# Summing 512 columns of A's part of the last row tile ahead of B's row tiles, and holding the sum in PSUM

## The chip, the cores and the metric

One core of a Trainium2 chip. The metric is the device time of one execution in microseconds; "span" is the same execution as the trace sees it, about 1.5 us shorter. TensorE does the matrix products and adds them up in PSUM, a memory of eight banks; ScalarE and VectorE read finished sums out of it (an "eviction") into SBUF, the working memory; the SyncE and ScalarE queues issue transfers (DMA).

## The reference, cut to what matters

```python
g = sigmoid((x * gate_w).sum(-1, keepdims=True))
a = linear_attention(x, A_wqkv, A_wo)      # 2048 x 640, 32 heads of 20
b = linear_attention(x, B_wqkv, B_wo)
return g * a + (1 - g) * b
```

Each attention block ends in a product with an output weight. The kernel folds each block's key-value sums into that weight (WPA, WPB, 640 x 640), so that its last stage is, for each of 16 row tiles of 128 rows, a product of scaled queries with WPA plus one with WPB.

## The kernel before

The output stage. `o_mm` adds one block's part of one row tile to PSUM: five contraction steps, each a 128x512 matmul and, for the full width of 640, a 128x128 one.

```python
def o_mm(X, t, ps, lo, hi, first="A", last="B"):
    ...
            for g in range(NC):                        # NC = 5
                for l0 in range(lo, hi, 512):
                    r = e.matmul(a[:, l0-lo : h0-lo], PQ[X, b][:, g, ...], WP[X][:, g, l0:h0],
                                 start=(X == first and g == 0), stop=(X == last and g == NC - 1))
    op("PE", fn, ..., ins=[bfx[X, b, t % 4 // 2]] + bwpm[X], outs=[ps], ...)   # waits for WP[X]

def o_part(t):      # A's part of a row tile, then ScalarE copies it to SBUF (OA)
    ps, b = Buf("oa", "ps", 2), Buf("oas")             # two PSUM banks
    o_mm("A", t, ps, 0, D, last="A")
    op("ACT", lambda e: e.activation(OA[t], psw(ps, D), ACT.Copy), ..., name="oac")

def o_rest(t):      # B's part, then VectorE adds OA and the row tile is stored
    ps = Buf("o", "ps", 2)
    o_mm("B", t, ps, 0, D, first="B")
    o_post(t, ps, 0, D, "ADD")
```

Row tiles 0 to 14 are done in these two passes, because WPB comes late: it is computed, stored to DRAM and loaded back in another layout. Row tile 15 is done in one go at the end, A and B into one sum:

```python
def out_last(t):
    for lo, hi, eng in ((0, 512, "ACT"), (512, D, "DVE")):
        ps = Buf("o", "ps")                            # one PSUM bank
        for X in XS:                                   # A, then B
            o_mm(X, t, ps, lo, hi)
        o_post(t, ps, lo, hi, eng, ...)

...
wp_burst("B", 0)
o_part(5)
o_part(6)
wp_burst("B", 1)      # second half of WPB; its store and the load follow
o_part(7)
for t in range(8, NOA):    # NOA = 15
    o_part(t)
...
for t in range(NOA):
    o_rest(t)
...
out_last(NT - 1)
```

A small scheduler inside the kernel orders the other engines' work and deals out the eight PSUM banks; TensorE's order is the program's.

## Time and profile before

| | us |
|---|---|
| time, median of the first three runs | 188.17 (188.03 to 188.83) |
| span of the profiled execution | 186.8 |
| TensorE busy | 184.0 (98%) |
| WPB: load issued, landed | 156.62, 161.35 |
| TensorE's first matmul of B | 161.49 |

The lines stand in the prediction below. Read them so: in a kernel whose TensorE is busy nearly all the time, look for the places where it stands still. Once it does so in the output stage, between A's last matmul and B's first, until WPB lands.

### The profile page before, as it was taken

Reading aid. Unit: us, or ns where it says so; the run is one execution under the profiler, and the core shown is the slowest. Engines: PE = TensorE matmul, PEld = TensorE weight load, DVE = VectorE, ACT = ScalarE, POOL = GpSimd, SP = SyncE. Lnnn points to the kernel's source line nnn. Section 1 sums busy time; section 2 is a strip of 40 time slices with the busy share of each in tenths; the row PEclk is TensorE's granted clock in tenths of the full one; section 3 lists DMA queues with packets and bytes.
Section 4 is the critical chain, followed back from the end, with each engine's and each line's share of the span. In section 5 each row is a group of like instructions: output and inputs, shape, how many; then the busy total and the mean of one; then the engine's idle time right before and its main releaser. Section 6 shows DMA issues by size and latency. Waiting matters only on the chain.

```text
span 186.8 us, 3273 instructions
## 1 busy us (share of the span) xinstructions
PE 184.0 (98%) x1297; PEld 106.6 (57%) x1297; DVE 137.4 (74%) x264; ACT 95.2 (51%) x167; POOL 0.8 (0%) x10
## 2 busy tenths in 40 slices
PE   9999999999999999999999999999999999999995
PEld 4555555555555556555557555555566555555552
DVE  2388888888833555487799999998899996368652
ACT  5455655556554546544675666887633775300001
POOL 1000000000000000000000000000000000000000
DMA  6999999994001011010701412025426256523433
GB/s 190 291 163 163 266 394 362 338 200 114 4 0 35 0 39 35 0 35 20 100 2 35 84 33 50 14 62 154 175 41 115 58 131 164 143 105 107 142 107 105
DMA packets 36501, 21.38 MB, mean 114 GB/s; under 512 B 25694, under 2 KB 36230, under 8 KB 36486
## 3 DMA queue, kind: packets, MB, share of 16 engines
q1 hardware_dynamic: 36044, 20.96, 44.4%
q8 instruction: 10, 0.16, 0.4%
q10 hardware_dynamic: 442, 0.21, 0.4%
q14 instruction: 5, 0.04, 0.1%
HBM read 10.87 MB, written 4.26 MB: 81 GB/s over the span
## 4 chain that ended last, share of the span: by engine, by line
PE 92%; DMA 4%; ACT 2%; issue 0%; DVE 0%; SPq 0%; DVEq 0%
PE ps L795 23%; PE ps L536 19%; PE ps L641 18%; PE ps L955 18%; PE ps L642 5%; PE ps L537 5%; DMA WPB<-wpsB 3%; DMA wpsB<-WKW 2%; PE ps L703 2%; PE ps L467 1%; ACT WKW L753 1%; PE ps L738 1%; ACT PKB L979 1%; PE ps L480 1%; DVE TSB L999 0%
## 5 line engine op out<-in xcount | busy, mean ns | idle before, releaser
L536 PE MATMUL ps<-WKW,XT 128*128 128x512 bf16 x160 | 44.6, 382 | 0.0
L812 ACT ACTIVATE EK<-ps 128x512 bf16<-128x512 f32 x40 | 23.9, 598 | 30.1 <-PE ps L795 29.9
L537 PE MATMUL ps<-WKW,XT 128*128 128x128 bf16 (+1 forms) x160 | 35.3, 220 | 0.0
L569 ACT ACTIVATE EK<-ps 128x640 bf16<-128x640 f32 x32 | 22.4, 704 | 10.3 <-DVE EK L572 5.4
L536 PEld LDWEIGHTS ps<-WKW,XT 128*128 128x128 bf16 x160 | 15.7, 98 | 19.6 <-DMA WKW<-in_B_wqkv_dram 0.7
L795 PE MATMUL ps<-XT,WQA 128*128 128x512 bf16 x100 | 24.5, 379 | 0.0
L795 PE MATMUL ps<-XT,WQB 128*128 128x512 bf16 x100 | 23.8, 380 | 0.0
L641 PE MATMUL ps<-XN,PKA 128*128 128x512 bf16 x80 | 23.5, 379 | 0.0
L641 PE MATMUL ps<-XN,PKB 128*128 128x512 bf16 x80 | 23.5, 379 | 0.0
L822 DVE TENSOR_SCALAR EK<-EK 128x512 bf16<-128x512 bf16 x40 | 11.6, 289 | 13.5 <-ACT EK L812 13.3
L642 PE MATMUL ps<-XN,PKA 128*128 128x129 bf16 x80 | 17.6, 220 | 0.0
L642 PE MATMUL ps<-XN,PKB 128*128 128x129 bf16 x80 | 17.6, 220 | 0.0
L955 PE MATMUL ps<-WPA,EX 128*128 128x512 bf16 x120 | 17.0, 299 | 0.0
L955 PE MATMUL ps<-WPB,PKA 128*128 128x512 bf16 x120 | 16.5, 299 | 0.3 <-DMA WPB<-wpsB 0.3
L795 PEld LDWEIGHTS ps<-XT,WQB 128*128 128x128 bf16 x100 | 10.9, 118 | 8.6 <-issue 0.4
L537 PEld LDWEIGHTS ps<-WKW,XT 128*128 128x128 bf16 x160 | 15.8, 98 | 0.0
L572 DVE TENSOR_SCALAR EK<-EK 128x640 bf16<-128x640 bf16 x32 | 10.4, 326 | 7.2 <-ACT EK L569 7.1
L795 PEld LDWEIGHTS ps<-XT,WQA 128*128 128x128 bf16 x100 | 10.6, 117 | 8.1
L641 PEld LDWEIGHTS ps<-XN,PKA 128*128 128x128 bf16 x80 | 9.4, 117 | 7.9
L641 PEld LDWEIGHTS ps<-XN,PKB 128*128 128x128 bf16 x80 | 9.4, 117 | 7.9
L580 DVE SCALAR_TENSOR_TENSOR PKA<-ps,EK 128x640 bf16<-128x640 f32 x16 | 13.2, 825 | 0.5
L580 DVE SCALAR_TENSOR_TENSOR PKB<-ps,EK 128x640 bf16<-128x640 f32 x16 | 13.2, 825 | 0.6
(77 smaller groups left out, 222.8 us busy)
## 6 DMA issues: line engine op xcount, KB each, us to landing
out_dram<-TSB SPq DMA_DIRECT2D x15, 160.0 KB, 1.8
XN<-in_A_x_dram SPq DMA_DIRECT2D x1, 2240.0 KB, 8.9
WKW<-in_A_wqkv_dram SPq DMA_DIRECT2D x5, 160.0 KB, 3.9
WKW<-in_B_wqkv_dram SPq DMA_DIRECT2D x5, 160.0 KB, 3.6
WQA<-in_A_wqkv_dram SPq DMA_DIRECT2D x1, 800.0 KB, 10.6
WQB<-in_B_wqkv_dram SPq DMA_DIRECT2D x1, 800.0 KB, 11.7
WVA<-in_A_wqkv_dram SPq DMA_DIRECT2D x1, 800.0 KB, 12.7
WVB<-in_B_wqkv_dram SPq DMA_DIRECT2D x1, 800.0 KB, 14.5
```

Source lines behind the costliest of these rows:

```text
L536: e.matmul(a[:, 0:512], l, WK[X][:, c, 0:512], start=(c == 0), stop=(c == NC - 1))
L537: return e.matmul(a[:, 512:w], l, WK[X][:, c, 512:w], start=(c == 0), stop=(c == NC - 1))
L569: op("ACT", lambda e: e.activation(EK[:, ek.slot, :], psw(ps, D), ACT.Exp), act_cost(D), ins=[ps] + first, outs=[ek], name="ke")
L572: lambda e: e.tensor_scalar(EK[:, ek.slot, :], EK[:, ek.slot, :], 1.0, EPS, op0=ALU.min, op1=ALU.add),
L580: lambda e: e.scalar_tensor_tensor(PKt[X][:, t, :], psw(ps, D), 0.0, EK[:, ek.slot, :], op0=ALU.max, op1=ALU.add),
L641: e.matmul(a[:, 0:512], l, XN[:, t, 0:512], start=(t == 0), stop=(t == NT - 1))
L642: return e.matmul(a[:, 512 : D + 1], l, XN[:, t, 512 : D + 1], start=(t == 0), stop=(t == NT - 1))
L703: r = e.matmul(PS[0:n, ps.slot, GR * i : GR * i + NC * w], WV[X][:, c, lo : lo + n], gv[:, c, :, 24 * u : 24 * u + w], start=(c == 0), sto ...
L795: r = e.matmul(PS[:, ps.slot, :], WQ[X][:, c, g::5], XT[:, c, 512 * b : 512 * b + 512], start=(c == 0), stop=(c == NC - 1),)
L812: lambda e: e.activation(EQ[:, eq.slot, :], PS[:, ps.slot, :], ACT.Exp),
L822: lambda e: e.tensor_scalar(EQ[:, eq.slot, :], EQ[:, eq.slot, :], 1.0, EPS, op0=ALU.min, op1=ALU.add),
L955: r = e.matmul(a[:, l0 - lo : h0 - lo], PQ[X, b][:, g, 128 * (t % 4) : 128 * (t % 4) + 128], WP[X][:, g, l0:h0], start=(X == first and g = ...
```

## The change

Its intent is to give TensorE something to do in that gap. A's part of row tile 15 needs no WPB; its 512-column piece is summed ahead of B's first row tile, and the sum stays in its bank until B's part is added.

```diff
-    def out_last(t):
-        for lo, hi, eng in ((0, 512, "ACT"), (512, D, "DVE")):
-            ps = Buf("o", "ps")
-            for X in XS:
-                o_mm(X, t, ps, lo, hi)
+    LAST = ((0, 512, "ACT"), (512, D, "DVE"))
+    blast = [Buf("o", "ps") for _ in LAST]
+
+    def last_a(t):
+        o_mm("A", t, blast[0], 0, 512)
+
+    def last_b(t):
+        for (lo, hi, eng), ps in zip(LAST, blast):
+            if hi == D:
+                o_mm("A", t, ps, lo, hi)
+            o_mm("B", t, ps, lo, hi)
             o_post(t, ps, lo, hi, eng, "ACT" if hi == D else "SP")
 ...
     for t in range(8, NOA):
         o_part(t)
+    last_a(NT - 1)
 ...
-    out_last(NT - 1)
+    last_b(NT - 1)
```

## The prediction

> **What bounds the kernel now.** I read the page's engine shares first, then the chain that ended last, then the waits in the last 30 us, and then the timeline around the two places that the diff touches. The page says that TensorE is nearly never free, and where the output matmuls (line 955) stand:
>
> ```profile
> PE 184.0 (98%) x1297; PEld 106.6 (57%) x1297; DVE 137.4 (74%) x264; ACT 95.2 (51%) x167; POOL 0.8 (0%) x10
> ...
> L955 PE MATMUL ps<-WPA,EX 128*128 128x512 bf16 x120 | 17.0, 299 | 0.0
> L955 PE MATMUL ps<-WPB,PKA 128*128 128x512 bf16 x120 | 16.5, 299 | 0.3 <-DMA WPB<-wpsB 0.3
> ```
>
> The last number of each row is idle time just before the group. A's output matmuls never wait. B's wait once, for the transfer that loads WPB, B's folded output weights. The chain that ended last, in order of time (start, us, what), passes through exactly that transfer:
>
> ```profile
> 152.88 3.61 DMA wpsB<-WKW
> ...
> 156.62 4.73 DMA WPB<-wpsB
> 161.35 0.14 issue
> 161.49 23.27 PE ps L955 x170
> ...
> 184.84 0.29 DVE TSB L999
> ```
>
> So the end is set by: WPB stored to DRAM and loaded back, landing at 161.35; 0.14 us until TensorE's first B matmul at 161.49; then TensorE without a pause to the last matmul; then an eviction and the last output transfer. Work that does not need WPB and can run before 161.49 is worth at most the hole that TensorE has there. How big is the hole? The views say 0.28, but that counts from a matmul's end. I take starts instead, from narrow cuts of the timeline (start, us, engine, line, operation, count):
>
> ```profile
> 160.99 0.22 PE L955 MATMUL ps<-WPA,PKA 128*128 128x128 bf16 x1
> ...
> 161.49 0.38 PE L955 MATMUL ps<-WPB,PKA 128*128 128x512 bf16 x1 [0.28 <-DMA WPB<-wpsB]
> ...
> 181.86 0.38 PE L955 MATMUL ps<-WPA,PKA 128*128 128x512 bf16 x1
> ```
>
> The first is the last matmul of A's row tile 14, the second the first of B's row tile 0, the third the first of the last row tile. Fifteen row tiles of five (512 + 128) pairs lie between the second and the third: 20.37 us, 1.358 a tile, 0.272 a pair.
>
> The end of the kernel in the timeline:
>
> ```profile
> 181.86 1.24 PE L955 MATMUL ps<-WPA,PKA 128*128 128x512 bf16 x5
> ...
> 182.94 1.24 PE L955 MATMUL ps<-WPB,GSA 128*128 128x512 bf16 x5
> 182.98 2.25 SPq L354 DMA_DIRECT2D out_dram<-TSB  x2
> ...
> 184.02 0.44 PE L955 MATMUL ps<-WPA,PKA 128*128 128x128 bf16 x5
> ...
> 184.28 0.60 ACT L1001 ACTIVATE TSB<-ps 128x512 bf16<-128x512 f32 x1 [22.32 <-PE ps L955]
> 184.30 0.44 PE L955 MATMUL ps<-WPB,GSA 128*128 128x128 bf16 x5
> 184.84 0.29 DVE L999 CAST TSB<-ps 128x128 bf16<-128x128 f32 x1 [1.89 <-PE ps L955]
> 185.17 0.35 ACTq L354 DMA_DIRECT2D out_dram<-TSB  x1
> ```
>
> From the starts 181.86 and 182.94: five 128x512 matmuls take 1.08 us of the stream, 216 ns each. From 184.02 and 184.30: five 128x128 take 0.28 us, 56 ns each.
>
> **What the Trainium skill says.** "TensorE: Matmul & The Clock Gate", section "Back-to-back issue gap", gives N/2.4 + 2.5 ns between warm matmuls: 216 ns at 512 columns, 56 at 128. The trace agrees with both to the nanosecond. (The same section names a faster sustained figure of about 131 ns at 512 columns; this trace does not show it.) "Perfetto Trace Analysis", section "Tensor Engine Instruction (MATMUL, LD_WEIGHTS)", says that a matmul's end is estimated by the profiler and only its start observed. The trace agrees: single 128x512 records last 379 ns while the next starts 216 ns later. That is why I measure the hole between starts. "PSUM — Partial Sum Buffer", section "The four PSUM rules", says that a group's first matmul clears the accumulate bits of the whole bank, so two groups open at once may not share a bank. That is the danger in leaving a sum open for 22 us; the kernel's own allocator, run without the chip, gives it bank 0 alone and the 128-column piece bank 1, while B's row tiles use the pairs 2-3, 6-7 and 4-5. No sum is broken.
>
> **The change part by part.** No instruction is added or removed: the built program has as many matmuls as before, the same instructions in the same order with the same waits on VectorE, ScalarE and the SyncE queue, and only TensorE's order and the PSUM banks differ.
>
> *Moved away from the end.* Five 128x512 matmuls (A's part of row tile 15, columns 0 to 511) leave the stretch 181.86 to 182.94. Everything after them comes 1.08 us earlier, counted from the start of B's first tile.
>
> *Put in front of B.* The same five stand right behind A's row tile 14. They need WPA and A's scaled queries, which tile 14 already used, and a free bank: bank 0 was last read by the ACT eviction of A's row tile 11, which the timeline has at 157.17 for 0.70 us, long done. Without a wait they can start one 128-wide slot after 160.99, at 161.05 (160.99 + 0.056), and B's first tile can follow at 161.05 + 1.08 = 162.13. WPB is there since 161.35, and with the 0.14 of issue B could have started at 161.49, so the wait for WPB vanishes altogether. B starts 162.13 - 161.49 = 0.64 later than before.
>
> *The sum.* -1.08 + 0.64 = -0.44 us. Equivalently: the gain is the hole, 161.49 - 161.05 = 0.44, since the moved piece (1.08) is longer than the hole. In general it is the smaller of 1.08 and the hole of that execution. The last-tile order behind the moved group stays (B's 512, A's 128, B's 128), so the ScalarE eviction (0.60), the VectorE copy (0.29) and the two output transfers keep their distance from the last matmul. 0.44 off 188.17 is 187.73, that is 0.23%.
>
> **The rivals.**
>
> *A PSUM wait in place of the DMA wait.* The held bank blocks its pair, so B's tiles rotate over three pairs in place of four, and tile n+3 must wait until VectorE's add of tile n has read its pair. Against it: tile 0 starts at 161.49 and three tiles later is 3 x 1.358 = 4.07 us on; its add ends here:
>
> ```profile
> 163.04 0.82 DVE L992 TENSOR_TENSOR TSB<-ps,XN 128x640 bf16<-128x640 f32 x1 [2.86 <-PE ps L955]
> ...
> 170.06 0.82 DVE L992 TENSOR_TENSOR TSB<-ps,XN 128x640 bf16<-128x640 f32 x1
> ```
>
> 163.86 is 2.37 after the tile's start, leaving 1.70 us. The worst is tile 5, held back by two query scalings of 0.81 us in VectorE's queue: it starts at 161.49 + 5 x 1.358 = 168.28, its add ends at 170.88, 2.60 later, leaving 1.47. So three pairs suffice. If I am wrong, say 0.2 us lost on two tiles, the gain is eaten: about 188.1.
>
> *The last outputs collide.* Row tile 14's store was issued at 182.98 and row 15's first one at about 184.90 (182.98 + 2.25 - 0.33 of its own issue), 1.92 apart. Now the first comes 0.64 later and the second 0.44 earlier, 0.84 apart, less than a store's 1.8 us from issue to landing in the page. For it: two transfers closer than before. Against it: earlier stores already go at 1.36 apart, and in a cut of the DMA engines after 182.98 they move tile 14's data only between about 183.8 and 184.35, from 0.8 to 1.4 after issue. Moved, that is 184.45 to 185.0, while row 15's data would begin at 184.46 + 0.8 = 185.26. No overlap; if the receipt alone is slow, perhaps 0.2 is lost: 187.9.
>
> *The hole is not what the profile shows.* The profile is one execution, and the landing of WPB is the least certain number in it: stores of 3.61 and a load of 4.73 us. If it lands 0.3 earlier in timed runs, the gain is 0.14 (188.03); if it lands 0.64 later or more, the gain is the full 1.08 (187.09). For a steady hole: the three times lie within 188.03 to 188.83, with two of them 0.14 apart.
>
> **Range and chances.** The centre is 187.73. The hole's uncertainty (0.14 to about 0.8) and the spread of the three runs before, mainly upward, give 187.3 to 188.2. Two per cent would be 3.76 us, more than three times the whole moved piece, so within 2% is near certain. Only a hidden stall in TensorE's stream could make it slower by that much, and nothing could make it faster by that much.
>
> **What would show each step.** Right: in the profile after, TensorE has no wait for WPB; the five A matmuls start near 161.05 and B's first near 162.13; the 15 tiles of B last 20.37 again; the last 128-column group starts near 183.86 in place of 184.30; the span is near 186.4. Wrong: VectorE named as a releaser of TensorE on line 955 after 162 (the PSUM rival); B's tiles as predicted but the last landing not 0.44 earlier (the output rival); a wait for WPB that remains although the five stand in front of it (WPB landed later than here).

## The result, and the profile after

The changed kernel took 188.27 us (median of six, 187.61 to 188.54); the kernel before, measured with it, 188.2 (188.03 to 188.83). The ratio is 0.9993, 95% interval 0.997 to 1.0016. (Ratios are the mean time of one kernel's runs over that of the other's in the same rounds, so not quite the ratio of these medians.) The predicted 0.9977 lies inside the interval, and 0.9993 of 188.17 is 188.04, inside the predicted range; the measured median itself lies 0.07 above its upper end. The timing alone can't tell whether anything was gained.

The trace can. The waits of TensorE, whole kernel, in the profile after (engine, tile, line, releaser, us, times, longest), without the first wait of 0.4 us on line 467, which both programs have:

```profile
PE ps L480 <- DMA XN<-in_A_x_dram: 0.3, 1, 0.3
PE ps L536 <- DMA WKW<-in_A_wqkv_dram: 0.3, 1, 0.3
```

The wait for WPB is gone, and no other on line 955 has come in its place. But two waits for input loads, at the start of the kernel, are new. They belong to no part of the change: the profile e1 below, of the kernel before, has both of them (0.2 each), and e2, of the changed kernel, has neither. The timeline after, at the places that the prediction named:

```profile
156.95 0.36 SPq L354 DMA_DIRECT2D WPB<-wpsB  x1
...
161.47 0.70 ACT L979 ACTIVATE XT<-ps 128x640 f32<-128x640 f32 x1 [0.65 <-PE ps L955]
162.34 16.46 PE L955 MATMUL ps<-WPB,PKA 128*128 128x512 bf16 x118
...
184.08 0.44 PE L955 MATMUL ps<-WPB,GSA 128*128 128x128 bf16 x5
184.63 0.29 DVE L999 CAST TSB<-ps 128x128 bf16<-128x128 f32 x1 [0.81 <-PE ps L955]
```

The line at 161.47 is ScalarE's eviction of A's row tile 14; before, it began at 161.25:

```profile
161.25 0.70 ACT L979 ACTIVATE XT<-ps 128x640 f32<-128x640 f32 x1 [0.65 <-PE ps L955]
```

So everything up to there was 0.22 later in the profile after. From that eviction to the start of the last group of matmuls it is 184.30 - 161.25 = 23.05 us before and 184.08 - 161.47 = 22.61 after: 0.44 shorter, as predicted. (This difference is the hole of that one execution of the kernel before; the table further down says how others compare.) I call this length **the stretch** from here on. Of the 0.44, 0.22 was lost before the stretch began, and the span fell by 0.2.

Where do the 0.22 come from? Follow one ScalarE instruction, the key exponential (line 569) that starts near 14.5 us, through profiles of both programs. Before, and after:

```profile
14.49 0.70 ACT L569 ACTIVATE EK<-ps 128x640 bf16<-128x640 f32 x1 [0.45 <-DVE EK L572]
```

```profile
14.71 0.70 ACT L569 ACTIVATE EK<-ps 128x640 bf16<-128x640 f32 x1 [0.45 <-DVE EK L572]
```

161.25 - 14.49 and 161.47 - 14.71 are both 146.76. The same holds in four more profiles taken below (14.98, 14.87, 14.40 and 14.54 us; evictions at 161.74, 161.63, 161.16 and 161.30). So in these six profiles the work between 14.5 us and the stretch takes the same time to 0.01 us, and the whole difference is made in the first 14.5 us, while the inputs are loaded. One profile below is an exception: in e7 it is 161.41 - 14.43 = 146.98, because near 104 us a weight load of TensorE waits for VectorE and the stream falls 0.22 behind. So the stretch can be compared between executions, while the time cannot without many rounds.

### The profile page after: what moved, and what is told of

Same layout as the page of the kernel before. It is cut to its first block, busy times and chain, and to the rows that moved or that the text cites. A ratio compares the mean times of both kernels' runs of the same rounds, so it can differ in the third digit from the quotient of the medians.

```text
span 186.6 us, 3248 instructions
## 1 busy us (share of the span) xinstructions
PE 182.1 (98%) x1272; PEld 106.7 (57%) x1297; DVE 137.4 (74%) x264; ACT 95.2 (51%) x167; POOL 0.8 (0%) x10
## 4 chain that ended last, share of the span: by engine, by line
PE 95%; DMA 2%; issue 1%; SPq 1%; DVE 0%; DVEq 0%
PE ps L955 23%; PE ps L795 23%; PE ps L641 18%; PE ps L536 17%; PE ps L537 5%; PE ps L642 5%; DMA WKW<-in_A_wqkv_dram 2%; PE ps L703 2%; PE ps L738 1%; SPq L354 1%; DVE TSB L999 0%; DVEq L237 0%
## 5 line engine op out<-in xcount | busy, mean ns | idle before, releaser
L536 PE MATMUL ps<-WKW,XT 128*128 128x512 bf16 x154 | 43.2, 381 | 0.3 <-DMA WKW<-in_A_wqkv_dram 0.3
L795 PE MATMUL ps<-XT,WQA 128*128 128x512 bf16 x96 | 24.0, 379 | 0.1
L955 PE MATMUL ps<-WPA,EX 128*128 128x512 bf16 (+1 forms) x117 | 16.7, 297 | 0.2
L955 PE MATMUL ps<-WPB,PKA 128*128 128x512 bf16 (+1 forms) x118 | 16.4, 298 | 0.1
```

Of the source, the lines that this page charges most:

```text
L536: e.matmul(a[:, 0:512], l, WK[X][:, c, 0:512], start=(c == 0), stop=(c == NC - 1))
L795: r = e.matmul(PS[:, ps.slot, :], WQ[X][:, c, g::5], XT[:, c, 512 * b : 512 * b + 512], start=(c == 0), stop=(c == NC - 1),)
L955: r = e.matmul(a[:, l0 - lo : h0 - lo], PQ[X, b][:, g, 128 * (t % 4) : 128 * (t % 4) + 128], WP[X][:, g, l0:h0], start=(X == first and g = ...
```

## The experiments

Two theories. **Theory 1**: the hole in front of B is 0.44 us as a property of the schedule, the change gains that, and the first timing hid it in noise. **Theory 2**: the hole depends on how long the load of WPB takes in an execution, the profiled one had a long load, and the mean gain is less. A rival to both: something at the end (held banks, closer output stores) takes gain back.

The size of the hole in a profile is the start of B's first matmul minus the moment when A's stream would have let it start. That moment is 0.205 us ahead of the start of the eviction of A's row tile 14 (161.25 - 161.045 in the first profile; 161.045 is the prediction's 160.99 + 0.056, there rounded to 161.05).

**The kernel before, again (e1).** No edit.

> The kernel before, unchanged, run against itself. It measures the noise: ratio 1.000, and how wide its interval is. The stretch from the start of ScalarE's eviction of A's row tile 14 (161.25 in the profile of before) to the start of the last group of 128-column matmuls (184.30) is 23.05 us in the first profile. Theory 1 (the hole is a fixed property of the schedule, gain 0.44): 23.05 again within 0.1. Theory 2 (the hole depends on the execution, and is often smaller than in the first profile, which is why the timed gain was 0.07% and not 0.23%): 22.6 to 22.9 here.

Measured: 188.65 us, ratio to the same program 1.0016 (0.9998 to 1.0033). That is the noise of this measurement: two copies of one program differed by 0.16%, with intervals as wide as the gain. In its profile:

```profile
157.16 0.36 SPq L354 DMA_DIRECT2D WPB<-wpsB  x1
...
161.74 0.70 ACT L979 ACTIVATE XT<-ps 128x640 f32<-128x640 f32 x1 [0.66 <-PE ps L955]
161.76 16.46 PE L955 MATMUL ps<-WPB,PKA 128*128 128x512 bf16 x117
...
184.57 0.44 PE L955 MATMUL ps<-WPB,GSA 128*128 128x128 bf16 x5
```

The stretch is 184.57 - 161.74 = 22.83, the hole 161.76 - (161.74 - 0.205) = 0.225. The load of WPB took 4.5 us from issue to landing in place of 4.7. This speaks for theory 2.

**The changed kernel, again (e2).** No edit.

> The changed kernel again with more rounds. Theory 1: ratio 0.9977 (0.44 of 188.2), the same stretch 22.61 us as in the first profile of after (161.47 to 184.08), no wait of TensorE for WPB; the first 0.9993 was noise that comes from before the stretch. Theory 2: ratio 0.999 to 1.000.

Measured: 188.06 us, ratio 0.9986 (0.9967 to 1.0005). In its profile (the last line: queue, count, KB, us from issue to landing):

```profile
161.30 0.70 ACT L979 ACTIVATE XT<-ps 128x640 f32<-128x640 f32 x1 [0.66 <-PE ps L955]
...
183.91 0.44 PE L955 MATMUL ps<-WPB,GSA 128*128 128x128 bf16 x5
...
WPB<-wpsB SPq DMA_DIRECT2D x1, 800.0 KB, 4.7
```

The stretch is 183.91 - 161.30 = 22.61 with no wait for WPB, though the load took 4.7 us here, against 4.5 in e1 on the same chip. The changed kernel has the same stretch whether the load takes 4.4 us (first profile after) or 4.7; the kernel before has not. The ratio lies between the two theories' figures and decides nothing.

**A wider hole, without and with the change (e3, e4).** In both kernels the second half of WPB is made one row tile of A later:

```diff
-    wp_burst("B", 1)
     o_part(7)
+    wp_burst("B", 1)
```

> The kernel before with the second half of B's folded weights made one row tile of A later, so that WPB lands later against TensorE's stream. The hole should grow by that tile, 1.36 us, from 0.44 to 1.80. Theory 1: the wait of TensorE for WPB about 1.6 in the list of waits (which counts from the modelled end), the stretch 23.05 + 1.36 = 24.41 us, time about +1.36 us or ratio 1.007 against before.

> The changed kernel with the same delay. Theory 1 (the gain is the smaller of the moved 1.08 us and the hole): the hole of 1.80 takes all of the moved piece, a wait of 0.7 (0.5 in the list of waits) for WPB stays, the stretch is 24.41 - 1.08 = 23.33 us, and the time is 1.08 us under that of e3_late_before: ratio against before 1.0015. Rival (something else at the end, the output transfers or the banks, takes back a part of any gain): the time falls by clearly less than 1.08, say 0.5, though the stretch falls by 1.08.

Measured: 190.81 us without the change (ratio to the kernel before 1.0151, 1.012 to 1.0183), 189.81 with it (1.0083, 1.0062 to 1.0103): 1.00 apart by the medians. (Two of the six runs of e3 took 192.1 and 192.3 and pull its mean up. The record gives a granted clock of 0.991 for these two and 1.0 for the other four; what lowered it is not known. The four have a mean of 190.74, 0.87 above the 189.88 of e4, with a standard error of 0.15.) B's first matmul, with its wait in brackets, and the last group, in e3:

```profile
163.74 16.46 PE L955 MATMUL ps<-WPB,PKA 128*128 128x512 bf16 x117 [2.44 <-DMA WPB<-wpsB]
...
186.55 0.44 PE L955 MATMUL ps<-WPB,GSA 128*128 128x128 bf16 x5
```

and e4:

```profile
163.70 16.46 PE L955 MATMUL ps<-WPB,PKA 128*128 128x512 bf16 x118 [1.43 <-DMA WPB<-wpsB]
...
185.43 0.44 PE L955 MATMUL ps<-WPB,GSA 128*128 128x128 bf16 x5
```

With evictions at 161.34 and 161.22 the stretches are 25.21 and 24.21: 1.00 shorter with the change, of 1.08 moved. The rest is not taken back at the end: B's first matmul stands 2.40 behind the eviction in e3 and 2.48 in e4, so WPB came 0.08 later there. From VectorE's last copy to the end of the span it is 2.02 us in e3 and 2.00 in e4. So where the hole is larger than the moved piece, the whole moved piece is gained in the stretch, and nearly all of it (0.87 to 1.00) in the time. The rival of a loss at the end falls.

The size of the hole was mispredicted. It grew by 2.16 (to 2.605), not by 1.36. The chain in e3:

```profile
154.34 4.31 DMA wpsB<-WKW
...
158.79 4.82 DMA WPB<-wpsB
163.61 0.14 issue
```

Its stores took 4.31 us where they took 3.61, its load 4.82 where it took 4.73. With the chain's start 1.37 later against the eviction, 1.37 + 0.70 + 0.09 = 2.16. I had moved the transfers and taken their durations as fixed.

**A fifth of the moved work (e5).**

```diff
+    def o_mm(..., gs=range(NC)):     # contraction steps to do
 ...
-        o_mm("A", t, blast[0], 0, 512)
+        o_mm("A", t, blast[0], 0, 512, gs=range(1))
-            if hi == D:
-                o_mm("A", t, ps, lo, hi)
+            o_mm("A", t, ps, lo, hi, gs=range(NC) if hi == D else range(1, NC))
```

> Only the first of A's five 128x512 matmuls of the last row tile is moved ahead (216 ns); the other four stay at the end. Theory 2 as it now stands (the gain is the smaller of the moved piece and the hole of that execution, which lay between 0.23 and 0.44 in two profiles of before): the stretch from the eviction of A's row tile 14 to the last group is 22.61 plus what the hole has over 0.216, that is 22.62 to 22.83, so half to all of the full change's gain from a fifth of its work. If instead each moved matmul gained its own time, the stretch would be one fifth of the way from before to after: about 22.9 to 23.0.

Measured: 188.03 us, ratio 0.9983 (0.9962 to 1.0005).

```profile
156.79 0.36 SPq L354 DMA_DIRECT2D WPB<-wpsB  x1
...
161.36 0.70 ACT L979 ACTIVATE XT<-ps 128x640 f32<-128x640 f32 x1 [0.66 <-PE ps L955]
161.38 16.46 PE L955 MATMUL ps<-WPB,PKA 128*128 128x512 bf16 x117
...
183.97 0.44 PE L955 MATMUL ps<-WPB,GSA 128*128 128x128 bf16 x5
```

The stretch is 22.61: one moved matmul gives what five give. WPB landed at 161.15 in the unrounded trace, so it was ready for B at 161.15 + 0.135 = 161.285, 0.13 behind A's end (161.36 - 0.205 = 161.155): a hole smaller than the 0.216 of one matmul. It is just outside the expected 22.62 to 22.83, because that range came from two holes of 0.23 and 0.44. A gain in proportion to the moved work, a fifth of this execution's hole, would have left 22.61 + 0.8 x 0.13 = 22.71 (the 22.9 of the expectation took a hole of 0.44), and is excluded, since the stretch otherwise repeats to 0.01.

**A's 128 columns as well (e6).**

```diff
-        o_mm("A", t, blast[0], 0, 512)
+        for (lo, hi, _), ps in zip(LAST, blast):
+            o_mm("A", t, ps, lo, hi)
-            if hi == D:
-                o_mm("A", t, ps, lo, hi)
```

> A's 128-column piece goes ahead as well (0.28 us more, 1.36 in all). The hole is already full: the stretch stays 22.61, no wait for WPB. At the end B's 512-column sum is finished 0.28 us later against the last matmul, so ScalarE's eviction starts about 0.26 after the last group's start in place of 0.02 before it, and its store becomes the last: span 0.0 to 0.15 us longer than with the change as it is. If more moved work gained more, the stretch would be 22.33.

Measured: 188.61 us, ratio 1.0017 (0.9997 to 1.0038), span 186.9. VectorE's last copy stands 184.54 - 161.38 = 23.16 behind the eviction, as in the changed kernel (184.63 - 161.47 = 23.16), so the stretch did not shorten further: a full hole can't be filled twice. But the tail from that copy to the end of the span is 2.34 in place of 2.01 (from unrounded times), 0.33 more where I allowed 0.15. The end of e6, with the landing of the last store in its last line (queue, count, KB, us from issue to landing):

```profile
184.87 0.38 ACTq L354 DMA_DIRECT2D out_dram<-TSB  x1
184.88 0.33 SPq L354 DMA_DIRECT2D out_dram<-TSB  x1
...
out_dram<-TSB ACTq DMA_DIRECT2D x1, 32.0 KB, 2.0
```

and of the changed kernel:

```profile
184.68 0.33 SPq L354 DMA_DIRECT2D out_dram<-TSB  x1
184.95 0.35 ACTq L354 DMA_DIRECT2D out_dram<-TSB  x1
...
out_dram<-TSB ACTq DMA_DIRECT2D x1, 32.0 KB, 1.6
```

There the two stores are issued 0.27 apart; in e6 they are issued within 0.01, and the 32 KB one lands after 2.0 in place of 1.6. The Trainium skill, "DMA: Bandwidth & Descriptors", section "Issuing engines are not separate DMA queues", says that transfers of different issuing engines run on the same 16 DMA engines and interleave; the longer landing agrees with that, though one profile of each is no proof that this is the cause. e5 took 188.03 and e7 (below) 187.89, so moving only the 512 columns, as the change does, looks the better choice.

**Two pairs of banks, and one (e7, e8).** The held sum takes four banks, then six:

```diff
-    blast = [Buf("o", "ps") for _ in LAST]
+    blast = [Buf("o", "ps", 4), Buf("o", "ps")]                # e7
+    blast = [Buf("o", "ps", 6, at=(0,)), Buf("o", "ps")]       # e8
```

> The changed kernel, but the held sum takes four banks in place of one, so that B's tiles rotate over two pairs of banks and not three. Tile n+2 waits for the add of tile n, which ended 2.39 us after the start of its tile (2.6 at worst, behind the query scaling), against 2 x 1.358 = 2.716. Theory (bank rivalry is harmless with room to spare): no or at most 0.2 us of waits of TensorE for VectorE in all, stretch 22.61 to 22.8, ratio against before 0.998 to 0.999. Rival (the held bank already costs something in the changed kernel, hidden in the gain): here it would cost several tenths on most tiles, 1 us or more.

> A control that must be slow: six banks held, one pair left for B's tiles. The next tile waits for the add of the one before it, so the pitch should be 2.39 plus about 0.06 for the wait, 2.45 in place of 1.358, over 14 tiles 15.3 us; the held sum itself waits about 0.9 for the eviction of A's row tile 14. Time about 188.1 + 16 = 204, with VectorE named as the releaser of TensorE on line 955: what the bank rival looks like when it is real.

Measured, e7: 187.89 us, ratio 0.9976 (0.9955 to 0.9997); stretch 184.02 - 161.41 = 22.61, no wait of TensorE on line 955. (The wait near 104 us that this profile alone has lies outside the stretch.) Two pairs are enough, so the three pairs that the change leaves cost nothing. Measured, e8: 204.98 us (two runs), near the expected 204. So it looks where the banks bind (the held sum itself also waited 0.8 for the eviction of A's row tile 14):

```profile
PE ps L955 <- DVE TSB L992: 13.7, 14, 1.0
```

**Two more looks at the kernel before (e9, e10).** No edit, one run each (their state is therefore unknown; only the stretch is used).

> A third profile of the kernel before, for the size of its hole alone. Theory 2 (the hole follows how long the load of WPB takes in that execution): stretch minus 22.61 is the hole, between 0.15 and 0.5, and it goes with the load's time from issue to landing: about 0.2 where that is 4.4 to 4.5, about 0.45 where it is 4.7.

> A fourth profile of the kernel before; the same expectation. If the hole did not follow the load's time, 4.7 would be seen with a hole of 0.2 or 4.4 with one of 0.45.

Measured, e9: load issued at 157.06, B's first matmul at 161.58, eviction at 161.63, last group at 184.39. And e10:

```profile
156.52 0.35 SPq L354 DMA_DIRECT2D WPB<-wpsB  x1
161.10 16.46 PE L955 MATMUL ps<-WPB,PKA 128*128 128x512 bf16 x120
161.16 0.70 ACT L979 ACTIVATE XT<-ps 128x640 f32<-128x640 f32 x1 [0.65 <-PE ps L955]
...
183.91 0.44 PE L955 MATMUL ps<-WPB,GSA 128*128 128x128 bf16 x5
```

B's first matmul starts ahead of the eviction of A's last tile in both: the hole is down to 0.15 and 0.14. All profiles together, but for e3 and e4 (other order) and e8 (banks bind); e6 is measured by VectorE's last copy:

| profile | load of WPB, us | stretch, us | stretch - 22.61 |
|---|---|---|---|
| before, first | 4.7 | 23.05 | 0.44 |
| before, e1 | 4.5 | 22.83 | 0.22 |
| before, e9 | 4.4 | 22.76 | 0.15 |
| before, e10 | 4.4 | 22.75 | 0.14 |
| changed, first | 4.4 | 22.61 | 0 |
| changed, e2 | 4.7 | 22.61 | 0 |
| one matmul moved, e5 | 4.4 | 22.61 | 0 |
| all of A moved, e6 | 4.5 | 22.61 | 0 |
| two pairs, e7 | 4.4 | 22.61 | 0 |

Theory 2 holds, with one correction. The hole of the kernel before varies, and its mean in four profiles is 0.24 us (e10's 0.14 lies just under the 0.15 that I had named as the least). It follows the landing, which is issue plus load, and not the load alone: the loads of e1 and e10 differ by only 0.02 (4.47 and 4.45, unrounded), but the load of e1 was issued 161.74 - 157.16 = 4.58 ahead of the eviction and that of e10 161.16 - 156.52 = 4.64, which is most of the difference between 0.22 and 0.14. The large step, from there to 0.44, is the load's (4.73); what makes a load long stays open.

A 0 in the last column does not mean that this execution had no hole to fill. How long it would have been can be estimated from the landing in the unrounded trace: landing plus 0.135 (the time to B's first matmul wherever it waited) minus the end of A's stream. This gives 0.26 for the changed kernel's first profile, 0.51 for e2, and 0.13, 0.32 and 0.16 for e5, e6 and e7. So a hole as long as the first one came again in e2, and the mean over all nine profiles is 0.26.

The timed runs agree: runs of the program before (34) have a mean of 188.40 us with a standard error of 0.06, the changed kernel's 12 have 188.14 with 0.09. That is 0.26 us or 0.14% less, with a 95% interval of about 0.04 to 0.48. So the timing alone would not exclude 0.44, and pooled over different chips, it is weaker evidence than the stretch. e5 and e7 are as fast as the change within noise; no version clearly beats it.

## Why the prediction was right or wrong

- *The hole is measured between starts, 0.44, not the 0.28 of the list of waits.* Right for that execution: the stretch shrank by 0.44 between the two first profiles. That they agree to 0.01 only says that the hole was read rightly; the first profile after had 0.26 to fill by the estimate above.
- *Moved piece 1.08, B delayed by 0.64.* Right. After, B starts 162.34 - 161.47 = 0.87 behind the eviction, before 161.49 - 161.25 = 0.24: 0.63 later, without a wait.
- *The gain is the smaller of 1.08 and the hole.* Right, shown from both sides: e4 gains 1.00 where the hole is larger, e5 all of it with 0.216 moved where it is smaller (0.13).
- *PSUM rival.* Rightly rejected: 1.47 us of slack at the worst tile was computed for three pairs, and even two pairs gave no wait.
- *Output-store rival.* Rightly rejected for the change: from VectorE's last copy to the end of the span it is 2.00 us before and 2.01 after.
- *"0.44 off 188.17 is 187.73."* This term was too large for the timed runs. The prediction named the landing of WPB as its least certain number, and worked out that a landing 0.3 earlier leaves a gain of 0.14. That rival came nearest: the profiled execution had the longest hole of the four, and the other three would have gained 0.14 to 0.22. It was wrong to centre on the one execution seen; the mean over nine is 0.26. That the predicted ratio still lies in the measured interval is luck of a wide interval.
- *"The last 128-column group starts near 183.86 ... the span is near 186.4."* Measured 184.08 and 186.6. The missing 0.22 is the later start (14.71 against 14.49), which the prediction did not consider at all.
- *"Within 2% is near certain."* Right, but it tests none of the steps: the whole moved piece, 1.08 us, is 0.6% of the time.

## What to carry to other kernels

Work moved into a wait gains the smaller of the work's length and the hole's, and the hole under a transfer is a distribution: one profile shows one draw of it. When the gain is of the size of the noise, measure between two instructions in the trace that bracket only the change, and check that the stream ahead of them is the same in every execution. When a held PSUM bank is feared, the test is cheap: hold more banks and see where TensorE starts to wait.

## What the Trainium skill lacked or had wrong

- "TensorE: Matmul & The Clock Gate", section "Back-to-back issue gap": the sustained figures for streams of weight load and matmul, about 131 ns at 512 columns and 81 ns at 128, do not fit here. Each matmul had its own weight load, and the spacing was 216 and 56 ns, as the same section's formula for isolated matmuls has it.
- "Perfetto Trace Analysis", section "Tensor Engine Instruction (MATMUL, LD_WEIGHTS)", says that ends are estimated, but not by how much idle time read from them is short: a 128x512 record lasted 379 ns at a spacing of 216, and the 128x128 one that ends A's stream 220 ns at a spacing of 56, so the hole of 0.44 us was listed as 0.28, and those of 0.14 to 0.22 not at all.
- "DMA: Bandwidth & Descriptors", section "Latency and other measured facts", gives no spread for one transfer repeated in the same program: the 800 KB load of WPB took 4.4 to 4.7 us in nine profiles of kernels with the same order of transfers.
- No page that I found gives the time from a transfer's landing, as the trace marks it, to the start of the engine that waits for it: TensorE's first matmul came 0.14 us after the landing in three profiles (161.35 to 161.49, 163.61 to 163.74, 163.56 to 163.70).
